# Attention weights transposed two groups behind their search, and routing steps regrouped, in a top-k attention plus mixture-of-experts kernel

## The chip, the core and the metric

The kernel runs on one core of a Trainium2 chip. A core has a matrix engine (TensorE, "PE" in the profile, its weight loads "PEld"), a vector engine (VectorE, "DVE"), a scalar engine (ScalarE, "ACT"), a general engine (GpSimd, "POOL") and a queue engine that mostly issues transfers (SyncE, "SP"). Each engine works through its own list of instructions in order, and they wait for each other on semaphores. The metric is device time in microseconds (us) of one execution, as the median of several runs.

## What is computed

The reference, cut to what matters:

```python
scores = scale * np.matmul(q, k.transpose(0, 1, 3, 2))        # 8 batches, 8 heads, 576 x 576, head_dim 64
kth    = np.partition(scores, -32, axis=-1)[..., -32:-31]      # the 32nd largest of each row
scores = np.where(scores >= kth, scores, -1e9)
attn   = softmax(scores)                                       # + 1e-9 in the divisor
x      = (attn @ v) as rows of 512                             # 4608 rows: 8 batches x 576
logits = x @ w_gate                                            # 8 experts, the largest one is taken
y      = relu(x_sorted[e] @ w1[e]) @ w2[e]                     # per expert: 512 -> 1024 -> 512
out    = gate_w[:, None] * y                                   # in the order of the rows again
```

All numbers are 32 bit floats.

## The kernel before

**Attention.** A *unit* is two heads of one batch, so there are 32 units, four per batch. Two neighbouring units make nine *groups*: four with two 128-row tiles of the first unit, one "tails" group with the 64-row ends of both units, four of the second. A batch has 18 groups, the whole attention 144. The loop `loop()` (L1162 to L1228) walks over the groups; for group i it does the following.

- DVE folds the scores of group i+1 (L306 `h`, L308 `l`, and, ahead of the last search round, L314 `few`, L316 `hl`: maxima and minima of halves) and searches group i for its 32 largest values: six MAX8 (L345), then four rounds of two MAX8 (L354), with two MATCH_REPLACE8 (L362) between rounds.
- ACT computes `low` (L371) from the 32nd value and a huge negative number for all scores below it (`depths`, L387, tile `w`); POOL subtracts it from the scores (`less`, L396, two instructions per group); ACT takes the exponential (`weights`, L404). POOL also keeps a note of doubtful rows (`doubts`, L377).
- PE transposes the finished weights (`transposed`, L415 and L429/L431) and ACT copies the transposes out of PSUM (L420, L422, L437, L439). Before the change this is `turning(i - 1)`: group i-1 is transposed while group i is searched. Three buffers hold `w`.
- PE computes the scores of group i+4 (`products`, L292); ACT copies those of group i+3 (L299).
- When a unit's last full tile has been passed, its *ending* begins (`ending`, L1045 on): a generator that runs a step at each named place of the loop ("products", "relu", "rows", "small", "weights", "turn", "pool"). It multiplies the weights with v (L452 `po`, copied at L454), turns the result into rows and logits (L463 `px`, copied at L470), takes the reciprocal of the softmax sums (L481 `rz`, after ACT at L474 to L479), and multiplies on POOL (L489 `xl`, L491/L492 `lg`, L502 `x`, 640 columns).

**Routing.** After the fourth unit of a batch the ending goes on: `choice` finds the largest logit (L512 to L522), `ranks` counts on PE (L533 to L536), `places` computes the row's destination (L548 to L558), five indirect transfers from POOL scatter the batch's rows to a buffer in DRAM (L569), and `table` (L613 to L653) lists which full blocks of 128 rows may now be worked on. These small DVE steps are generators put on the list `aside`; the function `tick()` runs the next one. The search calls `tick()` behind each MAX8 and MATCH_REPLACE8 of rounds r = 1, 2 and 3, which is up to ten steps per group.

**Experts.** A block is 128 rows of one expert: 16 *pieces* of PE work (L916, L933), plus a transpose (L811). In the loop a running `credit` says how many pieces are done in a group; `share` divides them between the tiles of a unit. The counts are fixed when the program is built. What is left after the attention is done at the end, four of the blocks as 192-row blocks (L852, L873, L888).

**Order.** PE, ACT and DVE run in the order in which the program is written (`manual_schedule`); on POOL the compute instructions keep the written order among themselves (`in_turn`), and a scheduler places the transfers. SP issues the loads of q, k, v, of blocks and of the experts' weights, and reads the block numbers of `table` on its own queue.

Of the kernel before, what the change touches and what calls it, by code (L numbers as in the profile page):

```python
# [19 lines left out]
NEG = -3.0e38  # L20
STEEP = 2.0 ** 120
EPS = 1e-9

# [19 lines left out]
def kernel(  # L43
# [154 lines left out]
    e_at = iota_f("e_at", [P, E], [[CAP, E]])  # L198
    slots = iota_f("slots", [1, NSLOT], [[1, NSLOT]])

# [14 lines left out]
    doubt = const.tile([P, B * U, NT, NL], F32, name="doubt")  # L215
    nc.gpsimd.memset(doubt, NEG)
# [7 lines left out]
    nc.vector.tensor_scalar_mul(done, e_at[0:1, :], 1.0 / P)  # L224
    slot_max = const.tile([1, 3], F32, name="slot_max")
# [3 lines left out]
    upto_all = const.tile([1, E + 1], F32, name="upto_all")  # L229
# [7 lines left out]
    blank = const.tile([P, XW], F32, name="blank")  # L237
    nc.gpsimd.memset(blank[:, 0:Dm + 1], 0.0)
    nc.gpsimd.iota(blank[:, Dm + 1:XW].bitcast(I32), pattern=[[0, 1]], base=N, channel_multiplier=0)
# [93 lines left out]
    def search(tiles, s, f, then=lambda: None):  # L333
# [16 lines left out]
        for r in range(R):  # L350
            if r == R - 1:
                then()
            for m in m_all:
                nc.vector.max(out=tops[:, m, r * 8:(r + 1) * 8], in_=src[m])  # L354
                if r:
                    tick()
            if r == 0:
                in_turn(nc.gpsimd.tensor_scalar_mul(nbias, tops[:, :, 0], -scale))
            if r < R - 1:
                for m in m_all:  # L360
# [5 lines left out]
                    if r:  # L366
                        tick()
# [5 lines left out]
        def doubts():  # L373
            n, i = tiles[0]
            at = n.b * U + n.u
# [7 lines left out]
    def depths(s, low):  # L383

        w = k.att.tile([P, 2, S], F32, name="w", bufs=1 if k.exact else 3)
# [118 lines left out]
    def choice(lg):  # L504
# [6 lines left out]
        def steps():  # L511
            nc.vector.tensor_reduce(mx, lg, axis=AX.X, op=ALU.max)  # L512
            yield
            nc.vector.tensor_tensor(oh, lg, _inner(mx[:, :], E), op=ALU.is_ge)
            yield
            nc.vector.tensor_tensor(oh, oh, _ins(e_less[:, :], 1, KC), op=ALU.mult)
            yield
            nc.vector.tensor_tensor(lg, lg, _inner(mx[:, :], E), op=ALU.subtract)
# [21 lines left out]
    def places(r, x):  # L540

        pos = k.small.tile([P, KC, E], F32, name="pos")
        posf = k.small.tile([P, KC], F32, name="posf")
# [3 lines left out]
        def steps():  # L547
# [4 lines left out]
            nc.vector.tensor_reduce(posf, pos, axis=AX.X, op=ALU.add)  # L552
            yield
            nc.vector.tensor_scalar_add(den, den, EPS)
            yield
            nc.vector.tensor_copy(r.posi, posf)
# [42 lines left out]
    def table(slot_i, n, last, riding=None):  # L599
# [3 lines left out]
        ci = sm.tile([1, E], I32, name="ci")  # L603
# [3 lines left out]
        upto, step = upto_all, step_all  # L607

        def steps():
            if last:  # L610
                nc.vector.tensor_scalar_add(full, run[0:1, :], float(P - 1))
                yield
            nc.vector.tensor_copy(ci, full if last else run[0:1, :])  # L613
            yield
            nc.vector.tensor_single_scalar(ci, ci, 7, op=ALU.arith_shift_right)
            yield
            nc.vector.tensor_copy(full, ci)
            yield
            if riding is not None:
                nc.vector.tensor_tensor(full, full, riding, op=ALU.subtract)  # L620
                nc.vector.tensor_tensor(full, full, done, op=ALU.max)
                yield
            nc.vector.tensor_tensor(left, full, done, op=ALU.subtract)
            yield
            nc.vector.tensor_tensor_scan(upto[:, 1:], ones[0:1, 0:E], left, 0.0, op0=ALU.mult, op1=ALU.add)
            yield
            nc.vector.tensor_tensor(step[:, 0:E - 1], done[:, 1:E], full[:, 0:E - 1], op=ALU.subtract)
            yield
            nc.vector.tensor_tensor(
                past[:, 0:n, :], _inner(slots[:, 0:n], E), _ins(upto[:, 1:], 1, n), op=ALU.is_ge  # L630
            )
            yield
            nc.vector.tensor_reduce(slot_f[:, 0, 0:n], past[:, 0:n, :], axis=AX.X, op=ALU.add)
            yield
            nc.vector.tensor_tensor(past[:, 0:n, :], past[:, 0:n, :], _ins(step[:, :], 1, n), op=ALU.mult)
            yield
            nc.vector.tensor_reduce(slot_f[:, 1, 0:n], past[:, 0:n, :], axis=AX.X, op=ALU.add)
            yield
            nc.vector.scalar_tensor_tensor(
# [738 lines left out]
```

## Time and profile before

| what | value |
|---|---|
| median of 3 runs | 1325.49 us (1323.74 to 1325.93) |
| the profiled execution | 1322.96 us |
| its span, first to last instruction | 1321.3 us |
| mean granted TensorE clock | 0.961 |
| busy: PE, PEld | 1194.3 us (90%), 838.0 us (63%) |
| busy: DVE, ACT, POOL | 1072.6 us (81%), 932.3 us (71%), 660.2 us (50%) |
| start of the first fold (`h`), end of the last search | 8.1 us, 1069.5 us |
| last expert matmul | 1293 us |

How to read the profile: the busy share of an engine is an average over the whole span. The kernel has a long stage, the attention with expert pieces between (to 1069.5 us), and a shorter one in which almost only PE works (to 1293 us). A row of a group has the line, the engine, the operation, the tiles (written<-read), the shapes, the number of instructions, their busy time, the mean duration of one in ns, and, behind the bar, the time the engine stood idle just before them, with what ended it. A row of the timeline has the start, the duration, the engine, the line and the instruction; a bracket at its end tells of idle time just before. Instructions of DVE overlap at their ends, so the time that one adds to the chain is a little less than its duration.

### The profile page before, as it was taken

What the parts mean: (1) busy time and instruction counts of PE and PEld (TensorE: products, weight loads), DVE (VectorE), ACT (ScalarE), POOL (GpSimd) and SP (SyncE); (2) the same over time, 40 slices, a digit from 0 to 9 for tenths busy, and PEclk for the clock granted to TensorE, in tenths of its full rate; (3) what the DMA queues carried; (4) which work ended last, traced back from release to release, by engine and by line L of the source; (5) the groups of instructions that cost most, each with busy time, mean ns of one, the idle gap of its engine ahead of it and who ended that gap; (6) DMA issues with size and microseconds to landing.
All of it is one profiled execution on the core that took longest, in us unless ns stands there. A gap on an engine that the chain in (4) does not pass through costs nothing. (4 is left out here: it accounts for less than half of the span.)

```text
span 1321.3 us, 24526 instructions
## 1 busy us (share of the span) xinstructions
PE 1194.3 (90%) x7654; PEld 838.0 (63%) x7654; DVE 1072.6 (81%) x4654; ACT 932.3 (71%) x2129; POOL 660.2 (50%) x806
## 2 busy tenths in 40 slices
PE   5767777898989899999999999999999999999995
PEld 3444444665666556666666666766676777699973
DVE  7999999999999999999999999999999943000000
ACT  4888878887898788888888888788878861111110
POOL 2454546554865485647564765575656642000000
PEclk9798887999999999999999999999999999999998
DMA  4000001841293029522955374447454659986580
GB/s 149 30 30 30 30 30 64 319 155 30 71 345 133 30 74 373 179 101 74 367 174 184 134 249 173 163 144 265 156 179 162 197 185 289 386 301 215 209 292 18
DMA packets 98509, 220.95 MB, mean 167 GB/s; under 512 B 5181, under 2 KB 25917, under 8 KB 98368
## 3 DMA queue, kind: packets, MB, share of 16 engines
q1 hardware_dynamic: 91664, 199.02, 43.1%
q0 software_dynamic: 6416, 19.97, 4.2%
q8 instruction: 62, 1.02, 0.3%
q14 instruction: 79, 0.65, 0.1%
q10 hardware_dynamic: 288, 0.30, 0.1%
HBM read 195.88 MB, written 24.17 MB: 167 GB/s over the span
## 5 line engine op out<-in xcount | busy, mean ns | idle before, releaser
L396 POOL TENSOR_TENSOR w<-s,w 128x576 f32<-128x576 f32 x288 | 410.5, 1445 | 412.8 <-ACT w L387 412.8
L916 PE MATMUL ph<-xTs,w 128*128 128x128 f32 x2112 | 261.2, 277 | 3.6 <-ACT xTs L813 3.6
L916 PEld LDWEIGHTS ph<-xTs,w 128*128 128x128 f32 x2112 | 249.6, 193 | 22.7 <-issue 18.0
L933 PE MATMUL py<-w,hT 128*128 128x512 f32 x528 | 249.6, 602 | 3.9 <-ACT hT L921 3.7
L404 ACT ACTIVATE w<-w,nbias 128x576 f32<-128x576 f32 x288 | 224.1, 792 | 4.8 <-POOL w L396 3.9
L387 ACT ACTIVATE w<-s,low 128x576 f32<-128x576 f32 x288 | 207.7, 768 | 4.7
L292 PE MATMUL sc<-qkb 64*128 64x288 f32 (+1 forms) x1280 | 200.7, 464 | 9.7 <-ACT s L299 5.1
L415 PE MATMUL wTm<-turn,w 128*128 128x128 f32 x1152 | 170.2, 288 | 32.1 <-ACT xl L470 15.8
L415 PEld LDWEIGHTS wTm<-turn,w 128*128 128x128 f32 x1152 | 133.3, 146 | 89.3 <-issue 32.3
L299 ACT COPY s<-sc 128x576 f32<-128x576 f32 x288 | 168.7, 639 | 10.0 <-PE sc L292 10.0
L1257 DVE CAST any_i<-pd 1x1 int32<-1x1 f32 x1 | 0.1, 146 | 201.1 <-PE pd L1255 201.1
L354 DVE MAX8 tops<-scr 128x8 f32<-128x168 f32 x576 | 163.1, 317 | 0.0
L422 ACT COPY wT<-wTm 128x512 f32<-128x512 f32 x256 | 139.1, 603 | 23.7 <-PE wTm L415 23.6
L354 DVE MAX8 tops<-few 128x8 f32<-128x144 f32 (+1 forms) x576 | 154.9, 301 | 0.0
L292 PEld LDWEIGHTS sc<-qkb 64*128 64x128 f32 (+1 forms) x1280 | 107.4, 191 | 71.0 <-issue 32.7
L933 PEld LDWEIGHTS py<-w,hT 128*128 128x128 f32 x528 | 92.4, 192 | 89.4 <-issue 83.5
L452 PE MATMUL po<-wT,vb 128*64 128x288 f32 x1024 | 148.1, 435 | 0.0
L345 DVE MAX8 few<-l 128x8 f32<-128x288 f32 x288 | 127.5, 443 | 0.0
L831 POOL DMA_INDIRECT out_dram<-y,xg x37 | 38.1, 1030 | 171.4 <-ACT y L892 76.5
L452 PEld LDWEIGHTS po<-wT,vb 128*64 128x64 f32 x1024 | 71.9, 145 | 71.8 <-issue 21.5
L306 DVE TENSOR_TENSOR h<-s 128x576 f32<-128x576 f32 x144 | 114.1, 792 | 2.5 <-ACT s L299 2.5
L308 DVE TENSOR_TENSOR l<-s 128x576 f32<-128x576 f32 x144 | 109.2, 758 | 0.0
(189 smaller groups left out, 1650.1 us busy)
## 6 DMA issues: line engine op xcount, KB each, us to landing
w<-in_moe_w_dram SPq DMA_DIRECT2D x74, 2048.0 KB, 9.2
qkb<-in_qk_dram SPq DMA_DIRECT2D x31, 608.0 KB, 4.0
vb<-in_v_dram SPq DMA_DIRECT2D x32, 320.0 KB, 3.3
xg<-x_rows SPq DMA_DIRECT2D x37, 257.0 KB, 9.1
x_rows<-blank SPq DMA_DIRECT2D x13, 257.0 KB, 5.4
x_rows<-blank POOLq DMA_DIRECT2D x4, 257.0 KB, 8.0
x_rows<-x,posi POOLq DMA_INDIRECT x40, 3.1
out_dram<-y,xg POOLq DMA_INDIRECT x37, 4.1
```

The lines of the kernel that those rows point to most:

```text
L292: nc.tensor.matmul(ps[rows, j, 0:HF], n.q[d, cols], n.k[d, keys], start=True, stop=True)
L299: lambda m=m, ps=ps: nc.scalar.copy(s[:, m, :, :], ps[:, :, 0:HF]) for m, ps in enumerate(got)
L345: nc.vector.max(out=f.few[:, m, QF + 8 * j:QF + 8 * j + 8], in_=away)
L354: nc.vector.max(out=tops[:, m, r * 8:(r + 1) * 8], in_=src[m])
L387: nc.scalar.activation(w[:, m, :], s[:, m, :, :].rearrange("p j k -> p (j k)"), AF.Relu, scale=-STEEP, bias=low[:, m:m + 1],)
L396: k.last_pool = in_turn(nc.gpsimd.tensor_tensor(w[:, m, :], s[:, m, :, :].rearrange("p j k -> p (j k)"), w[:, m, :], op=ALU.subtract)).ins
L404: nc.scalar.activation(w[:, m, :], w[:, m, :], AF.Exp, scale=scale, bias=nbias[:, m:m + 1], accum_out=n.z[:, c:c + 1])
L415: nc.tensor.transpose(pm[:, c * P:(c + 1) * P], w[:, m, first:first + P], ident)
L422: nc.scalar.copy(wT[:, :, m, q], pm4)
L452: nc.tensor.matmul(po[r, 0:HF], n.v[:, c, r], rhs, start=(c == 0), stop=(c == KC - 1))
L916: nc.tensor.matmul(ph[:, f, :], n.w1[:, 0, dt, fc * P:(fc + 1) * P], n.xT[:, dt, :], start=(dt == 0), stop=(dt == DT - 1),)
L933: nc.tensor.matmul(py, hT[:, f, :], n.w2[:, 0, f, :], start=(f == 0), stop=(f == FT - 1))
```

## The change

- **Lag.** `LAG = 2`: during the search of group i the weights of group i-2 are transposed. The unit's ending begins a group later (`ended(i + 1 - LAG)`). `w` gets a fourth buffer. After the loop two groups are left to transpose instead of one.
- **Pieces.** `share` is moved by one tile, so that the many pieces stay beside the same steps of the ending.
- **Routing steps.** `tick()` is called in rounds 2 and 3 only (six steps per group). `choice` has five steps for six (a subtraction first, then one fused instruction), `places` five for six (the sum is written as a whole number at once), `table` twelve for fifteen (rounding to whole blocks by adding a large number in place of two casts and a shift; one reduction for two). For the rounding ACT writes one more tiny tile per batch (`blocks`).
- **Order on POOL.** The places "pool", "relu" and "rows" of the loop now stand ahead of `put_stores()` and `scatter(1)`, which issue the transfers.
- **Doubts.** The note of doubtful rows is kept for two batches and reduced once per batch (`doubted`, 108 columns) instead of once at the end (864 columns).
- **Room.** The tile of blank rows is no longer kept in SBUF: it is made once in a block buffer (`xg`), copied to DRAM, and the fills at the end read it from there.

The diff, cut to its core:

```diff
@@ table and constants
+WHOLE = 1.5 * 2.0 ** 23
+UNDER = -127.0 / 256.0
-    doubt = const.tile([P, B * U, NT, NL], F32, name="doubt")
-    nc.gpsimd.memset(doubt, NEG)
+    doubt = const.tile([P, 2 * U, NT, NL], F32, name="doubt")
+    any_b = const.tile([P, B], F32, name="any_b")
-    blank = const.tile([P, XW], F32, name="blank")
+    blank = dram.tile([P, XW], F32, name="blank")
@@ search
                 nc.vector.max(out=tops[:, m, r * 8:(r + 1) * 8], in_=src[m])
-                if r:
+                if r > 1:
                     tick()
...
-                    if r:
+                    if r > 1:
                         tick()
@@ depths, load_half
-        w = k.att.tile([P, 2, S], F32, name="w", bufs=1 if k.exact else 3)
+        w = k.att.tile([P, 2, S], F32, name="w", bufs=1 if k.exact else 4)
@@ choice
-            nc.vector.tensor_tensor(oh, lg, _inner(mx[:, :], E), op=ALU.is_ge)
-            yield
-            nc.vector.tensor_tensor(oh, oh, _ins(e_less[:, :], 1, KC), op=ALU.mult)
-            yield
             nc.vector.tensor_tensor(lg, lg, _inner(mx[:, :], E), op=ALU.subtract)
+            yield
+            nc.vector.scalar_tensor_tensor(
+                out=oh, in0=lg, scalar=0.0, in1=_ins(e_less[:, :], 1, KC), op0=ALU.is_ge, op1=ALU.mult
+            )
@@ places
-            nc.vector.tensor_reduce(posf, pos, axis=AX.X, op=ALU.add)
+                nc.vector.tensor_reduce(r.posi, pos, axis=AX.X, op=ALU.add)
...
-            nc.vector.tensor_copy(r.posi, posf)
-            yield
@@ table
-            nc.vector.tensor_copy(ci, full if last else run[0:1, :])
-            yield
-            nc.vector.tensor_single_scalar(ci, ci, 7, op=ALU.arith_shift_right)
-            yield
-            nc.vector.tensor_copy(full, ci)
+                v.tensor_scalar(full, blocks, WHOLE, None, ALU.add)
...
-            nc.vector.tensor_reduce(slot_f[:, 0, 0:n], past[:, 0:n, :], axis=AX.X, op=ALU.add)
...
-            nc.vector.tensor_reduce(slot_f[:, 1, 0:n], past[:, 0:n, :], axis=AX.X, op=ALU.add)
+            v.tensor_reduce(slot_f[:, 1, 0:n] if last else slot_f[:, :, 0:n], both, axis=AX.X, op=ALU.add)
@@ around the loop
+    LAG = 2
...
-        for r in [e * CAP for e in range(E)] + [EMPTY * P]:
-            nc.sync.dma_start(x_rows[r:r + P, :], blank)
+        empty = k.mlp.tile([P, 1, XW], F32, name="xg", bufs=4)[:, 0, :]
...
+        for to in [x_rows[r:r + P, :] for r in [e * CAP for e in range(E)] + [EMPTY * P]] + [blank]:
+            nc.sync.dma_start(to, empty)
...
+        def doubted(b):
+            one = slice(b % 2 * U, (b % 2 + 1) * U)
+            nc.vector.tensor_reduce(any_b[:, b:b + 1], doubt[:, one], axis=AX.XYZ, op=ALU.max)
...
             nc.scalar.copy(run, r.run)
+            if b:
+                nc.scalar.activation(blocks, r.run[0:1, :], AF.Copy, scale=1.0 / P, bias=UNDER)
...
+        def ended(i):
+            b, g = work[max(i, 0)]
+            u, tile = g[0]
+            if i >= 0 and tile == NC - 1:
+                end = ending(b, u)
+                late.append([end, next(end)])
@@ loop
                 doubts()
-                put_stores()
-                scatter(1)
                 at_place("pool")
                 at_place("relu")
                 at_place("rows")
+                put_stores()
+                scatter(1)
                 at = i % per_batch
+                if at == LAG + 3 and b:
+                    doubted(b - 1)
...
-                share = {0: 0.5, 1: 1.2, 2: 1.6, 3: 0.5, 2 * NC: 1.4}[tile]
+                share = {0: (0.5, 1.4)[u % 2], 1: 0.5, 2: 1.2, 3: 1.6, 2 * NC: 0.5}[tile]
...
-                turns = turning(i - 1) if i else iter(())
+                turns = turning(i - LAG) if i >= LAG else iter(())
...
-                if tile == NC - 1:
-                    end = ending(b, u)
-                    late.append([end, next(end)])
+                ended(i + 1 - LAG)
                 at_place("products")
...
             k.between = True
+            for _ in turning(len(work) - 2):
+                pieces(1)
+            ended(len(work) - 1)
+            at_place("products")
             for _ in turning(len(work) - 1):
                 pieces(1)
```

## The prediction

> **What bounds the kernel now.** I read the busy time by stretches first, each stretch one batch of 18 groups, then the tail. (Columns: stretch, length, busy time and instructions of PE, PEld, DVE, ACT and POOL, granted clock, DMA share, GB/s.)
>
> ```profile
> 137.30:267.20 129.90, 100.00 (x613) 63.56 (x612) 129.90 (x577) 107.24 (x250) 73.86 (x93) 0.84 0.35 122
> 267.20:397.50 130.30, 117.92 (x788) 78.96 (x790) 130.30 (x572) 111.43 (x258) 80.54 (x96) 0.99 0.41 147
> 397.50:529.70 132.20, 120.09 (x785) 80.42 (x782) 131.71 (x572) 108.92 (x251) 79.20 (x93) 0.97 0.42 151
> 529.70:665.10 135.40, 131.28 (x884) 90.47 (x883) 133.19 (x572) 114.14 (x264) 85.18 (x100) 1.00 0.50 178
> 665.10:800.30 135.20, 132.32 (x893) 91.31 (x892) 134.99 (x573) 113.77 (x262) 83.01 (x99) 1.00 0.52 179
> 800.30:934.20 133.90, 131.59 (x897) 91.08 (x896) 133.34 (x572) 113.76 (x263) 82.48 (x95) 1.00 0.56 198
> 934.20:1069.50 135.30, 131.92 (x900) 91.73 (x899) 133.00 (x568) 113.89 (x264) 81.09 (x99) 1.00 0.50 173
> 1069.50:1110.00 40.50, 40.45 (x254) 29.11 (x253) 15.45 (x90) 14.02 (x35) 14.59 (x20) 1.00 0.67 226
> 1110.00:1293.00 183.00, 183.00 (x1102) 156.39 (x1101) 0.00 (x0) 32.18 (x53) 14.60 (x16) 1.00 0.78 275
> ```
>
> Number the batches 0 to 7; the rows begin with batch 1. In batches 1 to 3 DVE is never idle while PE idles 12 to 30 us: DVE sets the pace. In batches 4 to 7 both are nearly full; PE idles 4.1, 2.9, 2.3 and 3.4 us, 12.7 in all. From 1069.5 on PE has no idle time, so the tail's length is PE work. The end therefore comes earlier only by PE idle time that goes away.
>
> DVE is not always doing useful work in its busy time. An undisturbed group takes 6.92 us (`h` starts at 613.81 and again at 620.74), so 18 take 124.6. Batches 1 to 7 are longer by 5.3, 5.7, 7.6, 10.8, 10.6, 9.3 and 10.7 us. The timeline shows with what:
>
> ```profile
> 295.00 0.74 DVE L306 TENSOR_TENSOR h<-s 128x576 f32<-128x576 f32 x1
> 295.04 2.49 POOL L502 TENSOR_TENSOR x<-xl,rz 128x640 f32<-128x640 f32 x1
> 297.69 2.77 POOL L396 TENSOR_TENSOR w<-s,w 128x576 f32<-128x576 f32 x2
> 298.80 0.18 DVE L512 TENSOR_REDUCE mx<-lg 128x5 f32<-128x40 f32 x1
> 299.13 1.38 DVE L514 TENSOR_TENSOR oh<-lg,mx 128x40 f32<-128x40 f32 x1
> 300.74 0.18 DVE L516 TENSOR_TENSOR oh<-oh,e_less 128x40 f32<-128x40 f32 x1
> ```
>
> The same kind of step takes 0.18 us alone (L516) and 1.38 (L514) when it begins under POOL's `w` of 297.69 to 300.46: it ends as POOL ends. A reduction (L512) is not held. The folds are held too:
>
> ```profile
> 163.26 1.26 POOL L502 TENSOR_TENSOR x<-xl,rz 128x640 f32<-128x640 f32 x1
> 163.84 1.00 DVE L314 TENSOR_TENSOR few<-h 128x288 f32<-128x288 f32 x1
> ```
>
> against 0.44 us for L314 elsewhere. The groups by line give the sizes:
>
> ```profile
> L306 DVE TENSOR_TENSOR h<-s 128x576 f32<-128x576 f32 x144 | 114.1, 792 | 2.5 <-ACT s L299 2.5
> L314 DVE TENSOR_TENSOR few<-h 128x288 f32<-128x288 f32 x144 | 71.8, 499 | 0.0
> L481 DVE RECIPROCAL rz<-rz 128x10 f32<-128x10 f32 x32 | 6.3, 198 | 10.2 <-ACT rz L477 9.0 <-ACT rz L479 1.2
> L514 DVE TENSOR_TENSOR oh<-lg,mx 128x40 f32<-128x40 f32 x8 | 5.9, 732 | 0.0
> L613 DVE CAST ci<-run 1x8 int32<-1x8 f32 x8 | 5.2, 653 | 0.0
> ```
>
> Summing over the timeline what each DVE instruction adds to the chain beyond its undisturbed value gives, for batches 1 to 3 and 4 to 7: small routing steps 5.9 and 17.7 us (5.0 of the latter idle at L481, where the reciprocal comes before ACT's sums), folds 4.2 and 13.9. The small steps' own undisturbed share is 2.8 us a batch, 31 steps at 0.09.
>
> **The change part by part.**
>
> *Steps in rounds 2 and 3 only.* On time, `w` ends 4.05 us after `h` begins (608.03 + 2.83 against `h` at 606.82). Round 1 begins at +3.6, round 2 at +4.7. So in punctual groups the steps come behind `w`. In batches 1 to 3, 46 of 54 groups are punctual, and I take two thirds of 5.9: -3.9 us. In batches 4 to 7, `w` ends later than +4.7 in 36 of 72 groups, up to +8.0, because `low` on ACT is late by up to 4.9 us. There I take half of 17.7: -8.9. The reciprocal gains the same 1.1 us, which covers most of its five waits.
>
> *Fewer steps.* 31 become 27 a batch (five, five, twelve, four reciprocals, the new `doubted`): 4 x 0.09 = 0.36; with the smaller last reduction off the path, -1.1 in batches 1 to 3 and -1.4 in 4 to 7. The fused step has no row; its bounds are a fused table step (L639, 0.27 us) and the two steps it replaces (0.18 each), so nothing hangs on it. ACT's `blocks` costs about 0.2 us, as the copy beside it (L1093, 0.17), seven times; ACT is 84% busy, and if it is late there it adds at most 1.4 us to chains that PE bounds.
>
> A rule bears on that. The Trainium skill ("SBUF — State Buffer", section "Who interferes with whom") says that DVE and GpSimd share a port pair as an exclusive lock for a whole instruction, that the loser blocks fully, and that reductions never take part; L512 and L514 agree. It speaks against counting steps: one blocked step absorbs the whole of POOL's instruction, so merging steps saves only their own 0.09 us, and the sum would keep just the 2.5 us of this paragraph.
>
> *Rows ahead of transfers on POOL.* Where a transfer stands first, `x` runs later (295.04 here), holds no fold, but delays the next `w` to +5.5 and so holds the next steps. Moved forward, `x` stands at +5.1 to +6.4 as in the second excerpt and holds `few`, 0.56 us, in three units of a batch, and 0.22 in the first, whose `lg` is one instruction shorter: 1.9 a batch, 5.7 in batches 1 to 3 against 4.2 now: +1.5. The transfers queue behind: about 1.0 us each, ahead of the next `w`, which POOL has the idle time for (2.4 us before `w` at 608.03). Batches 4 to 7: no change taken.
>
> *Lag and fourth buffer.* In batches 4 to 7 no wait of PE on the exponential (L404) is among the waits; they are
>
> ```profile
> PE wTl L431 <- ACT wT L422: 6.3, 14, 1.1
> PE wTm L415 <- ACT oT L454: 1.7, 3, 0.8
> PE ph L916 <- ACT xTs L813: 1.3, 2, 0.6
> PE py L933 <- ACT hT L921: 1.1, 2, 0.6
> ```
>
> PSUM evacuations, which a longer lag leaves as they are. `w` is freed two groups before its reuse, as now. So zero; bounds: -12.7 (all PE idle time of these batches) and, as a loss, one wait of 3.8 us (the longest of ACT for transposes there, L420) in the first group. PE gets the same kinds and numbers of instructions; one group's transposes, nine at 0.11 us, move behind the loop, where exponentials are waited for anyway. SP's block numbers and loads come a group, 7 us, later; a block is first touched three groups after its loads are issued, and a load lands after 9.2 us, so they stay hidden. The blank rows read from DRAM: 5.4 to 8.0 us to landing now, in a tail with PE full; if slower by their own length, 8 us, still behind the three blocks of 14.5 us that PE does first.
>
> *Sum.* Batches 1 to 3: -3.9 - 1.1 + 1.5 = -3.5. Batches 4 to 7: DVE alone would give -8.9 - 1.4 = -10.3, but PE can give back at most 12.7 of idle time, in waits that are ACT's; I take half, -6.3. Tail 0. Total -9.8, so 1322.96 becomes 1313.2. The profiled run lies 2.5 us below the median of its runs; against the median the forecast is 1316 us.
>
> A rule against the limit by PE: the Trainium skill ("Perfetto Trace Analysis", section "Identifying the Most-Contended Engine") calls matmul busy time a bad measure and takes the weight loads' share. By it, 91 of 134 us, 68%, PE would have room, and the sum would be -3.5 - 10.3. In the tail, though, PE does nothing but wait for itself at 85%, and with wide matmuls (1120 to 1140 us) at 71%; 68% is full for such a mix.
>
> **The rivals.**
> - *All idle time closes*: `w` becomes punctual everywhere. -11 (steps 5.9 + 1.1, folds 4.2) and -12.7: -24, 1302 us. For it: everything held is held by late POOL. Against: groups with both v-products and expert pieces need over 9 us of PE (an estimate from the spacing of its matmuls, 0.11 to 0.43 us).
> - *Stalls only change place*: the rows hold `few` as often, late `w` the later steps; PE's idle time stays. -1 to -2: 1324. For it: ACT waits for PE in these batches. That the lag itself does nothing belongs here.
> - *Slower*: all steps now stand in the last third of a group, where a late `w` (to +8.0) lies. With 16 step groups in batches 4 to 7, each held 1.2 us, that costs 19.2 against 12.7 now (17.7 less the reciprocals' 5.0): +6.5, 1332 us. It decides from 11 of 16 groups late on; now half are.
>
> **How the numbers follow.** Forecast 0.50, all closed 0.15, change of place 0.22, slower 0.13. The range takes in the forecast (early -1 to -6, late -3 to -10), all closed, and change of place: 1302 to 1328. A measurement can tell 0.2%, 2.65 us. Faster: the first two and a little of the third, 0.67; same 0.20; slower 0.13.
>
> **What would show it.** Right: L514's successor and the first table step near 0.2 us; `few` held in most row groups; batches 1 to 3 shorter by 1 us each, 4 to 7 by 1 to 2; PE idle there 5 to 8 us; tail unchanged. Wrong: PE idle above 12.7, a wait of PE on L404's successor, batch 4 to 7 lengths unchanged, or idle time of PE after the last search.

## The result

Medians, each beside the kernel before on the same chip:

| kernel | median | ratio to before | 95% interval |
|---|---|---|---|
| before | 1324.03 us (1323.02 to 1325.93, 12 runs) | | |
| changed | 1323.48 us (1320.74 to 1327.64, 12 runs) | 0.9997 | 0.9984 to 1.0009 |

The change does nothing that can be measured; 1316 us was forecast. The profiled execution took 1323.02 us (span 1321.4). The stretches of its profile are cut where its own batches begin; columns as in the prediction.

```profile
136.50:269.20 132.70, 97.79 (x600) 61.34 (x602) 132.70 (x573) 106.45 (x249) 74.60 (x93) 0.86 0.31 110
269.20:398.00 128.80, 118.02 (x788) 79.57 (x784) 128.80 (x569) 110.44 (x258) 78.30 (x96) 0.97 0.41 146
398.00:527.30 129.30, 119.35 (x797) 80.08 (x796) 129.30 (x568) 111.93 (x260) 80.57 (x96) 0.99 0.46 165
527.30:659.60 132.30, 127.87 (x871) 88.72 (x871) 132.30 (x569) 112.48 (x262) 80.07 (x95) 1.00 0.50 180
659.60:797.30 137.70, 135.52 (x897) 92.14 (x896) 136.62 (x569) 115.02 (x266) 87.05 (x100) 1.00 0.51 177
797.30:930.10 132.80, 131.00 (x899) 91.43 (x897) 132.80 (x568) 115.15 (x267) 83.36 (x98) 1.00 0.58 199
930.10:1063.60 133.50, 131.84 (x901) 92.58 (x900) 133.44 (x564) 112.89 (x261) 85.09 (x96) 1.00 0.54 184
1063.60:1110.00 46.40, 44.05 (x275) 31.62 (x273) 14.52 (x86) 15.88 (x41) 15.28 (x23) 1.00 0.58 187
1110.00:1293.00 183.00, 183.00 (x1105) 156.66 (x1104) 0.00 (x0) 32.19 (x53) 14.86 (x17) 1.00 0.77 273
```

The first seven lengths add up to the good news: batches 2 and 3 are 1.5 and 2.9 us shorter, 4 to 7 together 3.5, batch 1 is 2.8 longer. With 0.8 us from before batch 1 the last search ends at 1063.6 instead of 1069.5, **5.9 us earlier**. The eighth row takes it back: behind the search, where PE had no idle time, PE is idle for 46.40 - 44.05 = 2.35 us. From the search's end to PE's last matmul, a tiny one behind the expert work, 236.6 us passed before and 242.1 now, **5.5 us more**. The last search and PE's last matmul, before and changed:

```profile
1068.96 0.55 DVE L354 MAX8 tops<-scr 128x8 f32<-128x168 f32 x2
1305.95 0.19 PE L1255 MATMUL pd<-ones,any_p 128*1 128x1 f32 x2
```

```profile
1063.01 0.56 DVE L359 MAX8 tops<-scr 128x8 f32<-128x168 f32 x2
1305.49 0.19 PE L1286 MATMUL pd<-ones,any_p 128*1 128x1 f32 x2
```

(PE's last expert matmul ends at 1306.0 before and 1305.6 now. The 1293 us in the table of times before is not PE's end: there a transfer starts, at 1293.01, that stands in the chain that ended last.)

The groups by line that answer to those of before (`h`, `few`, the reciprocal, and the two steps that took the place of L514 and L516):

```profile
L311 DVE TENSOR_TENSOR h<-s 128x576 f32<-128x576 f32 x144 | 110.2, 765 | 2.5 <-ACT s L304 2.5
L319 DVE TENSOR_TENSOR few<-h 128x288 f32<-128x288 f32 x144 | 77.9, 541 | 0.0
L486 DVE RECIPROCAL rz<-rz 128x10 f32<-128x10 f32 x32 | 6.2, 192 | 12.7 <-ACT rz L482 12.6
L519 DVE TENSOR_TENSOR lg<-lg,mx 128x40 f32<-128x40 f32 x8 | 3.4, 422 | 0.0
L521 DVE SCALAR_TENSOR_TENSOR oh<-lg,e_less 128x40 f32<-128x40 f32 x8 | 4.3, 540 | 0.0
```

`few` got dearer (499 to 541 ns), as the prediction said, and `h` cheaper (792 to 765). The reciprocal's 12.7 us lie almost all behind the search, where DVE sets nothing; up to 1062 us they are 0.3, against 4.5 before up to 1068 us. And the waits of PE in batches 4 to 7, then those behind the search (columns: total, times, longest):

```profile
PE wTl L436 <- ACT wT L427: 6.2, 12, 1.6
PE py L941 <- ACT hT L929: 1.1, 2, 0.6
PE wTm L420 <- ACT oT L459: 1.0, 1, 1.0
```

```profile
PE ph L924 <- ACT y L950: 1.2, 1, 1.2
PE wTl L436 <- ACT wT L427: 0.7, 1, 0.7
PE po L457 <- ACT wTt L444: 0.4, 1, 0.4
```

The largest, PE's wait for the transposes' evacuation, stayed: 6.3 before, 6.2 now. The second list is new: 2.3 us of waits in a tail that had none. Idle time of PE after the last search was one of the prediction's own signs of being wrong.

One place accounts for batch 1, whose tenth group takes 11.52 us where its neighbours take 7.3 and 7.5:

```profile
208.99 0.26 POOL L499 TENSOR_TENSOR lg<-xl 128x40 f32<-128x40 f32 x1
209.09 4.15 DVE L641 TENSOR_TENSOR past<-past,step_all 1x24 f32<-1x24 f32 x1
209.21 1.25 POOL L507 TENSOR_TENSOR x<-xl,rz 128x640 f32<-128x640 f32 x1
210.43 2.75 POOL L401 TENSOR_TENSOR w<-s,w 128x576 f32<-128x576 f32 x2
213.14 1.50 POOL L382 TENSOR_TENSOR doubt<-few,tops 128x6 f32<-128x6 f32 x1
213.18 0.74 DVE L311 TENSOR_TENSOR h<-s 128x576 f32<-128x576 f32 x1
```

A table step of 0.15 us (24 numbers on one partition) begins under POOL's `lg` and does not end with it: it lies through `lg`, `x` and both `w`, which follow each other without a pause, and costs 4.0 us.

### The profile page after: what moved, and what is told of

It reads as the page before. It is cut to its first block, busy times and chain, and to the rows that moved or that the text cites. A ratio compares the mean times of both kernels' runs of the same rounds, so it can differ in the third digit from the quotient of the medians.

```text
span 1321.4 us, 24464 instructions
## 1 busy us (share of the span) xinstructions
PE 1192.6 (90%) x7654; PEld 837.0 (63%) x7654; DVE 1070.7 (81%) x4625; ACT 933.6 (71%) x2136; POOL 661.5 (50%) x806
## 5 line engine op out<-in xcount | busy, mean ns | idle before, releaser
L941 PE MATMUL py<-w,hT 128*128 128x512 f32 x528 | 246.7, 598 | 2.1 <-ACT hT L929 2.1
L420 PE MATMUL wTm<-turn,w 128*128 128x128 f32 x1152 | 168.9, 286 | 26.8 <-ACT oT L459 10.8
L457 PE MATMUL po<-wT,vb 128*64 128x288 f32 x1024 | 152.0, 444 | 0.4 <-ACT wTt L444 0.4
L359 DVE MAX8 tops<-few 128x8 f32<-128x144 f32 (+1 forms) x576 | 150.8, 300 | 0.0
L311 DVE TENSOR_TENSOR h<-s 128x576 f32<-128x576 f32 x144 | 110.2, 765 | 2.5 <-ACT s L304 2.5
```

Source lines behind the costliest of these rows:

```text
L420: nc.tensor.transpose(pm[:, c * P:(c + 1) * P], w[:, m, first:first + P], ident)
L457: nc.tensor.matmul(po[r, 0:HF], n.v[:, c, r], rhs, start=(c == 0), stop=(c == KC - 1))
L941: nc.tensor.matmul(py, hT[:, f, :], n.w2[:, 0, f, :], start=(f == 0), stop=(f == FT - 1))
```

## The experiments

The first question was whether both halves of the change do nothing, or two effects cancel; e1 to e4 ask it, and their letters mean what their texts say. The answer (they cancel) gave **theory A**, which most of e5 to e18 test: the lag, costed at nothing, costs what the steps gain, because it leaves PE work undone while DVE paces and has it done behind the search, where PE paces. Its **rivals**: B, a lag of two makes PE wait more in the early batches; C, the shifted `share` is what costs; D, the late batches or the chain behind the search get longer. E, F and G are small ones of single runs. All runs in one table; "search" is the end of the last search, "rest" the time from there to PE's end, both from the profiled run; "hold" says whether the table step of batch 1 is held for 4 us or more.

The search's end has to be read with care, since it is that of one execution. Up to the last group of batch 6 e17 is the same program as the changed kernel, and its profile begins that group at 926.0 us, that of the changed kernel at 923.2. So a difference of up to 3 us between two search ends shows nothing by itself. The column "rest" repeats much better.

| run | median us | ratio [95%] | search | rest | hold |
|---|---|---|---|---|---|
| changed kernel | 1323.5 | 0.9997 [0.9984, 1.0009] | 1063.6 | 242.1 | yes |
| e1 lag alone | 1330.6 | 1.0060 [1.0040, 1.0080] | 1070.6 | 241.8 | no |
| e2 steps alone | 1317.3 | 0.9956 [0.9943, 0.9969] | 1063.7 | 236.6 | yes |
| e3 steps from round 1 | 1333.5 | 1.0081 [1.0068, 1.0094] | 1073.8 | 241.8 | no |
| e4 rows first | 1319.5 | 0.9975 [0.9966, 0.9983] | 1061.2 | 242.1 | no |
| e5 steps, rows first | 1314.8 | 0.9945 [0.9931, 0.9959] | 1062.0 | 236.6 | no |
| e6 old share | 1361.1 | 1.0291 [1.0277, 1.0306] | 1101.9 | 242.2 | yes |
| e7 lag 2, 1 from batch 4 | 1318.6 | 0.9973 [0.9964, 0.9982] | 1064.7 | 236.6 | yes |
| e8 lag 1, 2 from batch 4 | 1319.6 | 0.9986 [0.9974, 0.9998] | 1058.6 | 242.1 | no |
| e9 place alone | 1319.2 | 0.9970 [0.9960, 0.9981] | 1065.7 | 236.6 | no |
| e10 steps, old POOL order | 1313.8 | 0.9932 [0.9918, 0.9945] | 1060.0 | 236.6 | no |
| e11 more DVE early | 1345.5 | 1.0160 [1.0146, 1.0174] | 1086.5 | 242.1 | yes, and one each in batches 2 and 3 |
| e12 more DVE late | 1332.4 | 1.0062 [1.0049, 1.0076] | 1074.5 | 241.1 | yes |
| e13 changed, old POOL order | 1323.9 | 1.0003 [0.9994, 1.0012] | 1064.8 | 242.1 | no |
| e14 lag 2 from batch 1 | 1325.4 | 1.0015 [1.0006, 1.0025] | 1066.5 | 242.1 | yes |
| e15 lag 2 from batch 7 | 1320.9 | 0.9978 [0.9969, 0.9987] | 1062.6 | 241.3 | yes |
| e16 fewer steps alone | 1321.8 | 0.9993 [0.9984, 1.0002] | 1067.4 | 236.6 | no |
| e17 lag 2, 1 in batch 7 | 1320.1 | 0.9977 [0.9964, 0.9991] | 1067.7 | 236.9 | yes |
| e18 late lag 2, old order | 1318.8 | 0.9970 [0.9958, 0.9981] | 1061.5 | 241.4 | no |

The column "rest" already tells the main thing. It falls into two bands: 236.6 to 236.9 in every kernel that ends with a lag of one, 241.1 to 242.2 in every one that ends with two, whatever else was changed.

### The two halves: e1, e2

e1 is the kernel before with LAG, `share`, the fourth buffer, the blank rows in DRAM and the doubts per batch; e2 is the changed kernel without the first three (cut to the lag):

```diff
-    LAG = 2
...
-                turns = turning(i - LAG) if i >= LAG else iter(())
+                turns = turning(i - 1) if i else iter(())
...
-                ended(i + 1 - LAG)
+                if tile == NC - 1:
+                    end = ending(b, u)
+                    late.append([end, next(end)])
```

> Theory A (only PE idle time that goes away shortens the kernel, and the lag alone takes none away): no wait of PE on the exponential existed, so the kernel before with the lag, the fourth buffer, the moved shares and the blank rows in DRAM, but the old routing steps, stays at 1324 us, within 2 us. Rival B (the lag costs time: the DVE gain of the whole change, 5.9 us at the end of the search, is eaten by it): 1327 to 1331 us, with PE idle time grown behind the search or in batch 1. Rival C (the lag brings the gain, the steps nothing): 1319 to 1321 us.

> The changed kernel with the old lag of one, the old shares and three buffers. Theory A: the steps alone shorten batches 1 to 3 by 4 to 6 us unless one long hold as in batch 1 of the changed kernel (4.0 us at the table's multiplication) falls in again; 1319 to 1321 us without a hold, 1323 to 1325 with it. Rival B: 1317 to 1320 us whatever the holds. Rival C: 1324 us.

Each half moves by its own amount: the steps' edit by -0.44% (5.8 us), the lag by +0.60% (7.9 us), and on top of the steps by 0.9997 - 0.9956 = 0.41%, 5.4 us. Two effects cancel. (Both runs lie where the B of their texts puts them, 1327 to 1331 and 1317 to 1320.) In the profiles the steps alone and the whole change finish searching 0.1 us apart (1063.7 and 1063.6); only the rest differs. Here is the stretch behind the search, first of e2, then of the changed kernel:

```profile
1063.70:1100.00 36.30, 36.24 (x233) 26.28 (x232) 14.53 (x87) 13.01 (x34) 13.50 (x17) 1.00 0.64 212
```

```profile
1063.60:1100.00 36.40, 34.05 (x206) 23.27 (x204) 9.31 (x56) 13.88 (x38) 13.14 (x19) 1.00 0.46 161
```

PE is idle for 0.06 and for 2.35 us. The rest of the 5.5 is work. PE's groups by line from 1063.65 to 1110, the three that differ in number and are not expert work (e2, then the changed kernel):

```profile
L420 PE MATMUL wTm<-turn,w 128*128 128x128 f32 x16 | 2.3, 278 | 0.0
L468 PE MATMUL px<-turn,oT 128*128 128x144 f32 x10 | 1.8, 307 | 0.1
L436 PE MATMUL wTl<-turn,w 128*128 128x128 f32 x3 | 0.8, 274 | 0.0
```

```profile
L420 PE MATMUL wTm<-turn,w 128*128 128x128 f32 x24 | 3.5, 275 | 0.0
L468 PE MATMUL px<-turn,oT 128*128 128x144 f32 x20 | 3.1, 296 | 0.1
L436 PE MATMUL wTl<-turn,w 128*128 128x128 f32 x4 | 1.1, 286 | 0.7 <-ACT wT L427 0.7
```

Behind the search stand eight more `wTm`, one more `wTl`, and ten more `px`: besides the postponed group's nine transposes a second unit's turn into rows, since the unit's ending comes a group later too. Taken without their overlaps all PE work of the rest is 239.8 against 236.6 us; the three lines give 2.8 us of that. So +5.5 = 3.2 of work and 2.3 of idle time: A's work put off, and of D the chain.

### The pieces: e6

```diff
-                share = {0: (0.5, 1.4)[u % 2], 1: 0.5, 2: 1.2, 3: 1.6, 2 * NC: 0.5}[tile]
+                share = {0: 0.5, 1: 1.2, 2: 1.6, 3: 0.5, 2 * NC: 1.4}[tile]
```

> The changed kernel with the old table that shares the expert pieces out over a unit's five groups; lag two stays. Theory A (the lag's +6 us come from work put off to the stretch where PE has no idle time, so the share has nothing to do with it): 1323 us, within 1.5. Rival C (the shift of the pieces that came with the lag is what costs; the lag by itself is nothing): 1317 to 1318 us, PE idle 103 instead of 108.6.

Both answers miss: it costs 38 us, in the opposite direction to rival C. In batches 4 to 7 the first group of each nine, where the `px` of a unit's row turn stand, takes 8.89 us on average (7.64 in the changed kernel): more expert pieces now fall into the same group as the row turn, which is the likely cause but was not isolated. PE's waits there:

```profile
PE wTl L436 <- ACT wT L427: 17.8, 20, 2.0
PE wTl L434 <- ACT wT L425: 7.2, 4, 2.8
```

25.0 us against the 6.2 of the changed kernel. That is 18.8 of the 38 us; the remainder was not taken apart (some 11 us of the 38 lie in batches 1 to 3). The shifted `share` belongs to the lag: without it the lag costs not 0.4% but 3.3%.

### Where the lag is paid: e7, e8, e14, e15, e17, e18

`turning` and `ended` follow a counter, so that the lag changes on the way; `share` follows it. The switches stand at groups 71, 79, 25, 133 and 125, in the order of the runs (e18 is e8 with the old order on POOL). e7 and e17 go from two to one, as shown; the others go from one to two. The code is cut:

```diff
+                lag = 2 if i < 71 else 1
...
-                turns = turning(i - LAG) if i >= LAG else iter(())
+                fresh = next_t <= i - lag
+                if next_t < i - lag:
+                    for _ in turning(next_t):
+                        pass
+                    next_t += 1
```

> The changed kernel with a lag of two groups up to the end of batch 3, one group from there on (the postponed group is caught up in the first group of batch 4); share follows the lag, four weights buffers. Theory A (work put off to the end costs, since PE idles early and not late): the group is caught up where PE has idle time, so most of the cost goes: 1317 to 1319 us. Rival B (a lag of two makes PE wait more in the early batches): the cost stays, 1322 to 1324. Rival D (what costs is the chain in the late batches, an evacuation that comes later): cost goes too, 1317; it is told from A by the next kernel.

> The mirror image: a lag of one group up to the eighth group of batch 4, two groups from there on to the end. Theory A in its plain form (2.5 us of PE work are put off past the last search, whenever the lag begins): the work is put off here too, but out of a stretch where PE idles only 1 to 4 us a batch, so it costs at most that: 1318 to 1320 us. Rival D (the lag makes late batches or the chain behind the search longer): 1322 to 1324 us, with PE idle of batches 5 to 7 above 5 us. Rival B (early batches): 1317.

> The changed kernel with a lag of one up to the eighth group of batch 1, then two to the end. The earlier switch, in batch 4, left the end of PE 4.9 us earlier than with two from the start (medians 1319.6 against 1322 to 1323.5). Theory A: here the switch lies where DVE sets the pace, so the work that is put off (3.2 us) leaves only idle time behind it and nothing ends earlier: 1321.5 to 1323.5 us, the last search no earlier than 1062.5. Rival G (the lag costs in the first groups, where the pipeline fills): 1317 to 1319 us.

> The same with the switch at the eighth group of batch 7. Theory A: PE sets the pace there, so the search ends earlier by about the 3.2 us of PE work that are put off behind it, and only the 2.3 us of idle time behind the search are added: 1318 to 1320 us, last search near 1060.5, rest behind it 242.1. Rival (the whole 5.5 us longer rest is the cost, wherever the lag begins): 1322 to 1324 us, last search at 1063.7.

> The changed kernel with a lag of two up to the end of batch 6 and one in batch 7. In every run so far the time from the last search's end to PE's end was 236.6 us where the lag at the end was one, 241.1 to 242.2 where it was two, of it 2.3 idle. If the cost is paid there (theory A): rest 236.6, the group is caught up while PE sets the pace, so the search ends 1 to 3 us later than the changed kernel's 1063.6; 1318 to 1321 us. Rival B (early stalls of a lag of two): 1323 us.

> Steps with the old order on POOL (1313.8 with a lag of one, last search 1060.0; 1323.9 with a lag of two from the start, last search 1064.8), with a lag of one up to the eighth group of batch 4 and two from there. None of the three has the table step that is held for 4 us in batch 1, which the runs with the switch in batches 4 and 7 differed in. Theory A (a late switch puts off work that PE had no room for, so the search ends earlier by 1 to 3): last search 1057 to 1059, rest 242.1, 1316 to 1319 us. Rival (all 5.5 are paid wherever the lag begins): last search 1060, 1319.5 us. If 1322 or more, the old order and a lag of two collide late, not early.

e7 and e17 have a lag of two through all the early batches, and PE has no idle time behind the search (their stretches, e7 first):

```profile
1064.70:1110.00 45.30, 45.24 (x269) 31.45 (x268) 14.54 (x87) 14.35 (x37) 15.58 (x21) 1.00 0.70 250
```

```profile
1067.70:1110.00 42.30, 42.24 (x259) 29.88 (x257) 14.53 (x87) 14.09 (x36) 15.54 (x21) 1.00 0.71 249
```

With a rest of 236.6 and 236.9 they are faster than the changed kernel by 0.24% and 0.20%, 3.2 and 2.6 us of the 5.4. So B, under which the whole cost would stay, falls: about half goes when the last stretch has a lag of one again. What still parts them from the steps alone (0.9973 and 0.9977 against 0.9956, 2.3 and 2.8 us) lies before the search's end and is not explained. (e17's runs lie between 1316.6 and 1325.3, so its median is loose.)

The second half of A, that a lag beginning late is cheap because the search ends earlier, did not hold up well. Each is best compared with a lag of one that has the same held step and, where there is one, the same order on POOL: e15 with e2, e8 with e5, e18 with e10. The ratios differ by 0.22%, 0.41% and 0.38%, that is 2.9, 5.4 and 5.0 us, each uncertain by some 2 us: in one of three pairs part of the cost comes back, in two hardly any. (The comparison of e8 with e2 would look better for A, but 4 us of it are the held step, which e2 has and e8 has not.) The search ends themselves, 1.1 and 3.3 us earlier and 1.5 later, do not settle it: the profiled run of e8 lies 1.9 us below the median of its runs and that of e18 1.2 above. By their texts e15 falls between its two answers (1320.9); e18 has A's time (1318.8, which is near the rival's 1319.5 too), but its search ends later than either said. e14, where the lag begins in batch 1, is as slow as the changed kernel or slower (1325.4, above A's 1321.5 to 1323.5); rival G falls with it, and why it is slower is open.

What is shown is this: every kernel that ends with a lag of two has 4.4 to 5.6 us more behind the search. What the lag does before that differs from kernel to kernel. By the medians it costs 5.4 us on top of the steps, 7.9 on the kernel before (e1, which has the blank rows in DRAM and the doubts per batch as well), and 9.4 on top of e10 (e13).

### The steps taken apart: e3, e9, e16, e10, e13, e4, e5

e9: only the place, on the kernel before (`if r:` becomes `if r > 1:`, twice); e3: the reverse on the changed kernel; e16: only the smaller number of steps, on the kernel before. e10 and e13 put the old order on POOL back into e2 and into the changed kernel:

```diff
                 doubts()
+                put_stores()
+                scatter(1)
                 at_place("pool")
                 at_place("relu")
                 at_place("rows")
-                put_stores()
-                scatter(1)
```

e4 (changed kernel) and e5 (e2) pin the order, so that the scheduler can't put a transfer ahead of `x`:

```diff
-        in_turn(nc.gpsimd.tensor_tensor(xu, xl, _inner(rzb, D), op=ALU.mult))
+        k.last_pool = in_turn(nc.gpsimd.tensor_tensor(xu, xl, _inner(rzb, D), op=ALU.mult)).ins
```

> The changed kernel with routing steps run from round 1 again (ten per group). Theory A: L519 and the first table steps come under a punctual w again in row groups alone; batches 1 to 3 lose about 2 to 4 us, and the total is 1325 to 1328 us, unless the hold in batch 1 goes with it, then 1322 to 1324. If the round does not matter (the rival): 1323.5 us and the same sum of held small steps.

> The kernel before with one edit: routing's steps stand in rounds 2 and 3 of the search only (two conditions r become r > 1). The lag, the number of steps, the order on POOL stay as before. Theory A (the steps' place is the gain; undoing it in the changed kernel cost 10 us): 1314 to 1317 us against 1323.5, PE idle 98 to 103. Rival E (the gain of the steps edit comes from fewer steps and from the order on POOL, and the place matters only when a lag of two makes groups late): 1321 to 1323 us.

> The kernel before with fewer steps only: the steps stay in rounds 1 to 3, the order on POOL and the lag stay as before. The prediction gave this edit -1.1 in batches 1 to 3 and -1.4 at most in 4 to 7: 1321 to 1322.5 us. By subtraction on the runs (steps with the old order -9.2, the place alone -4.0) it is -5: 1318 us.

> The kernel of the steps alone (1317.3: lag one, steps fewer and later, rows ahead of the transfers) with the order on POOL put back as before: the transfers queued ahead of the row operations. The prediction priced the new order at +1.5, so by it 1315.5 to 1316. Theory F (a transfer ahead of x makes x and the next w late; pinning rows first gained 2 to 4): 1318 to 1321 us.

> The changed kernel with the order on POOL put back as before (transfers queued ahead of the row operations); lag two and the other steps edits stay. On top of the lag of one that edit alone was worth 3.5 us (1317.3 to 1313.8). If the parts add up: 1319.5 to 1320.5 us, the distance to the 1313.8 again the lag's 5.5 to 6. Rival (with a lag of two the new order is needed, since the late rows then share their group with more work): 1323 us or more.

> The changed kernel, with the transfers bound to come after the rows on POOL (in the changed kernel the scheduler still puts scatter and store ahead of the first unit's rows). Theory A: the hold of 4.0 us in batch 1 and those of about 1 us at L657 in batches 4 and 5 go, x ends at +6.1 us of its group; batch 1 is 3 to 4 us shorter, the total 1318 to 1321 us. Rival (a hold only moves to another step or fold, or PE's later batches absorb it): batch 1 shorter, total 1322 to 1324 us.

> The changed kernel with the lag back at one group (old share, three weights buffers) and, new, with the order on POOL pinned so that a batch's transfers stand behind its row multiplications. So far, against 1323.5 for both kernels: the steps alone 1317.3, the pinned order on top of the changed kernel 1319.5, that is -4.0 there. Theory A (steps, lag and POOL order act on different things and add up): 1317.3 - 4.0 = 1313 us, PE idle before the last matmul 98 to 100 us. Rival (the pinned order only repairs what the lag of two spoils): 1317 us, as the steps alone, PE idle 102 to 103.

Undoing the place in the changed kernel costs 0.84% (11 us, e3), more than either answer said, although e3 has not the held step of batch 1. On the kernel before the place alone gives 0.30% (4.0 us), the number alone 0.07% (0.9, not told apart from nothing), so e9 falls between its two answers, and e16 is as the prediction had it. Together they give 0.68% (9.0 us, e10): the parts help each other, and why is open. **e10, at 1313.8 us, is faster than both kernels.** Its distance to e2 is 0.24%, 3.2 us (3.5 between the medians). In the profiles it is 3.7 us, of which batch 1 alone gives 3.8 (129.6 against 133.4 us); what lies ahead of it and batches 2 and 3 give 1.8 more, and 4 to 7 take 1.8 back. At the place of batch 1 where e2 and the changed kernel have the held step e10 shows

```profile
202.06 0.27 POOL L499 TENSOR_TENSOR lg<-xl 128x40 f32<-128x40 f32 x1
202.29 2.63 POOL L507 TENSOR_TENSOR x<-xl,rz 128x640 f32<-128x640 f32 x1
202.31 0.15 DVE L641 TENSOR_TENSOR past<-past,step_all 1x24 f32<-1x24 f32 x1
202.39 0.74 DVE L311 TENSOR_TENSOR h<-s 128x576 f32<-128x576 f32 x1
```

where the same step begins 0.25 us after `lg` began instead of 0.10, takes its 0.15 us, and it is now POOL's `x` that takes 2.63 us where 1.25 is usual. Theory F ("a late `x` costs") fell with this run. The order's price is put down to this one collision and some longer `few` (L319 is busy for 73.7 us in e10, 77.3 in e2); the batches fit that, but no run removes the collision alone. e5 has the new order, pinned, without the collision and stands between the two, 1314.8, as between its two answers; e4 gains 0.22% on the changed kernel, as its theory A said, and it too is without the collision.

With a lag of two the old order wins nothing (e13, 1323.9), though the hold is gone; that is its rival's number, and the parts don't add up. Against the changed kernel e13's profile is 1.8 and 0.7 us shorter in batches 1 and 2, 1.0 and 3.9 longer in 3 and 4, and 1.2 shorter in 5. Why is open. The granted clock from 240 to 260 us is 1.00 in the changed kernel, e10 and e18, 0.82 in e13, 0.71 in e14 and 0.70 in e17; but it is 0.83 in e4 too, whose search ends early, and the 3.9 us of batch 4 come later, at a mean clock of 0.99.

### Which engine paces: e11, e12

```diff
+        if not k.exact and 1 <= tiles[0][0].b <= 3:
+            for _ in range(1):
+                nc.vector.max(out=spent, in_=scr[:, 0, :])
```

behind the last search round of the changed kernel (e12: `4 <= ... <= 7`); the output is not used. (It reads 168 columns, by the rows below, not the 138 of e11's text.)

> The changed kernel with one more MAX8 over the 138 reduced values (0.24 us) behind the search of every group of batches 1 to 3, its result unused: 54 x 0.24 = 13.0 us more DVE work where the theory says that DVE sets the pace. Theory A: nearly its full price, 1333 to 1337 us. Rival (PE work sets the end everywhere and DVE's time early is made up later): under +5, 1328.

> The same MAX8 in every group of batches 4 to 7 instead: 72 x 0.24 = 17.4 us more DVE work. Theory A (there PE sets the pace, and DVE's held steps and idle time, some 15 us, take it up): +3 to +8, 1326 to 1331 us. Rival (DVE sets the pace there as well, both engines full): +15 or more, 1338 us.

The added instructions in the two profiles:

```profile
L377 DVE MAX8 spent<-scr 128x8 f32<-128x168 f32 x54 | 16.7, 309 | 0.0
```

```profile
L377 DVE MAX8 spent<-scr 128x8 f32<-128x168 f32 x72 | 22.2, 309 | 0.0
```

Early, 54 times 0.24 us added to the chain (0.31 less the overlap of 0.07), 13.0 us, moved the search's end by 22.9 and the time by 1.63% (21.6 us) over the changed kernel: more than full price, and above the answer of A. In this profile two more table steps were held, 4.7 us each; the first:

```profile
347.23 1.87 POOL L576 DMA_INDIRECT x_rows<-x,posi  x1 [0.17 <-issue]
348.70 4.85 DVE L663 TENSOR_TENSOR done<-done,left 1x8 f32<-1x8 f32 x1
349.13 0.27 POOL L503 TENSOR_TENSOR lg<-xl 128x40 f32<-128x40 f32 x1
349.36 1.26 POOL L511 TENSOR_TENSOR x<-xl,rz 128x640 f32<-128x640 f32 x1
350.58 0.23 POOL L364 TENSOR_SCALAR nbias<-tops 128x2 f32<-128x2 f32 x1
350.77 2.75 POOL L405 TENSOR_TENSOR w<-s,w 128x576 f32<-128x576 f32 x2
```

13.0 + 2 x 4.7 = 22.4. Late, 17.4 us of the same work cost 0.65% (8.6 us), half its price and a little above A's +3 to +8. So DVE paces batches 1 to 3 in full, as the prediction read from the stretches, and 4 to 7 only in part.

## Why the prediction was wrong

**The step that failed** is the lag "so zero", with the sentence "one group's transposes, nine at 0.11 us, move behind the loop, where exponentials are waited for anyway". In its place: +5.5 us behind the search and +5.4 in the time, outside its bounds of -12.7 and +3.8. Three things were wrong in it. The count: nine transposes move, as it says, but ten `px` move with them: the prediction took no account of the unit's ending, which comes a group later too. The cover: the prediction had itself shown that PE has no idle time behind 1069.5, so nothing is "waited for anyway" there; moved work counts in full, 3.2 us. And the chain: the last unit's transposes, evacuations and row turn now stand behind one more group, and PE waits 2.3 us for ACT in it.

**The sum, term by term**, by the ratios of e10, e2 and the changed kernel:

| term | predicted us | measured us |
|---|---|---|
| routing steps, place and number (e10, with the doubts and blank rows) | -11.3 | -9.0 |
| order on POOL (e2 against e10) | +1.5 | +3.2 |
| lag, `share`, fourth buffer (changed against e2) | 0 | +5.4 |
| total | -9.8 | -0.4 |

The lag is 5.4 of the 9.4 us that the forecast missed; the other two terms were mis-sized by 4.0. That e2, without the lag, has 1317.3 us and the forecast was 1316 is luck: the forecast started from 1325.49, the kernel before beside e2 has 1323.27, and e2 gains 5.8 us where 9.8 were forecast.

**Steps.** Predicted without the order's term: -5.0 in batches 1 to 3, -6.3 in 4 to 7. e10, which has these edits, has -5.5 and -3.1 (and -0.9 ahead of batch 1) in its profile. The early term was right; of the late one half came. In the changed kernel, where these batches gain 3.5, PE's idle time in them went from 12.7 only to 10.1 us (5 to 8 was given as a sign of being right), and the wait for ACT's evacuations, which the prediction had named as the limit, stayed at 6.2.

**Place and number** were split as -3.9 and -1.1 early; over all batches they give 4.0 and 0.9 alone, and 9.0 as a pair. The split was not a sum.

**Order on POOL.** +1.5 was predicted for `few` being held; measured is +3.2 with a lag of one. The longer `few` is seen (3.6 us of busy time), but in the profile 4.0 us come from one held table step, which the prediction did not have. The Trainium skill ("SBUF — State Buffer", section "Who interferes with whom") was cited with an exclusive lock per instruction, under which the loser blocks fully. The trace agrees on single collisions: L521 takes 0.18 to 0.20 us in five of eight cases and 1.10 to 1.14 in three. But the prediction priced a collision at one instruction of POOL, and the step at 209.09 was held through four in a row.

**Fourth buffer, blank rows, fused step.** No wait for a free buffer of `w` appears in the profile after. For the blank rows POOL waits once, 3.5 us ahead of a store at 1115 us, in a stretch in which PE is never idle; e2 has the same blank rows and the rest of the kernel before, 236.6 us. Nothing speaks against the zeros given.

**Rivals.** "Stalls only change place", 1324 us, has the right time for the wrong reason: the steps did gain, and a place that it didn't name took it back. It did say that the lag itself does nothing. No case had a real gain and a real loss of the lag together.

**The share** was not priced at all. e6 shows that it is the condition under which the lag costs only 5.4.

**Open**: why place and number help each other; why the lag costs 5.4 on top of the steps, 7.9 on the kernel before and 9.4 with the old order on POOL; how much of its cost returns when it begins late; why the hold's absence is worth nothing in e13. That the order of the pieces of work behind the search could be changed so that the 2.3 us close was not tried.

## What to carry to other kernels

- A longer lag in a software pipeline leaves one more step of everything for the end. Price it at the end first: list each instruction that is left over, and if the engine that runs them has no idle time there, they cost in full, plus the longer chain.
- Cut the time at the last instruction of the pacing engine and compare "until then" and "from there" between kernels. Here the two halves of a null result came apart in one subtraction, -5.9 and +5.5, and the second part stayed within 0.3 us among all kernels that end with a lag of one, and within 1.1 among those that end with two.
- Before two experiments are subtracted, look whether a single rare event of some us stands in one of them and not in the other. Here it was one instruction of 4 us, as much as the effect looked for. Look also how far the same code repeats: two profiles of it were almost 3 us apart by the end of batch 6 here.

## What the runs showed of the hardware

- A DVE instruction of 0.15 us was held for 4.0 us, through four instructions of POOL that followed each other without a pause (`lg`, `x`, `w`, `w`), and another for 4.7 us, through the end of a transfer's preparation and the five that followed, in e11. The first hold stands in nine of the twenty kernels, and in all nine the step begins 0.1 us after `lg`. In e10 and e13 it begins 0.24 us after `lg`; there it takes 0.15 us, and POOL's next instruction takes 2.63 us instead of 1.25.
- The same code can repeat closely in two profiles: in batches 1, 2 and 3 PE is idle for 34.9, 10.8 and 9.9 us in the changed kernel and in e7. But it need not: e17 runs the same code there too, with a granted clock of 0.70 against 1.00 from 240 to 260 us, and its batch 1 is 134.2 us long against 132.7.
